# A convolution and MLP backward pass on one Trainium2 core: jobs read operand by operand, a constant burst at the front, diagonals on GpSimd, and new engine orders

## The chip, the core and the metric

The kernel runs on one core of one Trainium2 chip. A core has a matrix engine (TensorE, PE in the profile; its weight loads are PEld), a vector engine (VectorE, DVE), an engine for functions of single elements (ScalarE, ACT), a general one (GpSimd, POOL) and one that here only issues transfers (SyncE, SP). Matmul results arrive in PSUM, everything else lies in SBUF, and DMA engines move data between SBUF and the chip's memory. DMAs are issued from the instruction streams of SP, POOL and ACT, in order. The metric is the time of one execution in microseconds on the device; lower is better. Three runs of the kernel before gave 709.86, 711.56 and 712.73, a median of 711.56 us.

## The reference: what is computed

Two layers of each of two kinds are applied to x = A_q, (S, D) = (2048, 448), F = 1792; then the whole is differentiated. The outputs are the result and the gradients for eight inputs.

```python
def _A_ref(q, k, v, shift_k, ssm_k, ssm_D):
    # k_shift: causal convolution of k over 4 positions, per channel
    kv = k_shift * v
    # y: causal convolution of kv with ssm_k over all 2048 positions, by FFT of length 4096
    y = y + kv * ssm_D
    return q * y

def _B_ref(x, w1, w2):
    return silu(x @ w1) @ w2

x = A_q
x = x + _A_ref(_layernorm(x), A_k, A_v, A_shift_k, A_ssm_k, A_ssm_D)
x = x + _B_ref(_layernorm(x), B_w1, B_w2)
x = x + _A_ref(_layernorm(x), A_k, A_v, A_shift_k, A_ssm_k, A_ssm_D)
x = x + _B_ref(_layernorm(x), B_w1, B_w2)
# outputs: x, and the gradients of A_q, A_k, A_v, A_shift_k, A_ssm_k, A_ssm_D, B_w1, B_w2 for a given grad_out
```

The convolution's result y depends on k, v and the filters alone, so both A layers share one y: it is computed once, ahead of everything that depends on x.

## The kernel before

The work has three parts.

**Head** (`Head.run`, 0 to about 84 us). It computes y. The filter (ssm_k) arrives as four blocks of rows (L364, tiles K_sb and KK), is transposed on TensorE (L427, PSUM tile ps_kt) and copied out; then sixteen pairs of 128x448 matmuls with the Fourier matrix M1 (L456, ps_s) give the first FFT stage, and casts bring the results into A1K. In between, k is transposed (L444, ps_kT), and its 4-tap convolution is done as matmuls (L510) with diagonal matrices, sixteen 112x112 tiles, which VectorE makes from the identity and the taps skc (L414). The FFT of kv, the product and the inverse follow. The copies out of PSUM, of lines L92 (ScalarE) and L94 (VectorE), go to whichever of the two the planner picks.

**Flow** (`Flow.tile`, about 84 to 460 us). Sixteen tiles of 128 rows each go through two MLPs forward and two backward: norm (n0), gate, norm (n1), the turn of n1, up-projection (L663, ps_h), SiLU and its derivative (L700), down-projection (L726, ps_o), norm, gate, norm (n3), the second MLP with output, and then back: gradient up (ps_g), product with the derivative (ghp, ghT), down (ps_n), norm backwards, twice. A tile's stages are spread over many tiles' time, so several tiles are in flight. An operand is "turned" (128 rows by 448 columns transposed) either by two DMA transposes issued on SP (L636, L637) or, for the pairs listed in `ON_PE`, by four TensorE transposes into PSUM (L645) and one copy. The activations and gradients (A0, A1, GH0, GH1) are stored to memory for the weight gradients: A0 and A1 by a DMA transpose and a store on SP (L717, L718), GH0 and GH1 by one store on SP (L711).

**Tail** (from about 460 us). The backward FFT (L875 transposes, L903, L917, L923) gives the gradients for k, v and the filters (`Tail.ends`), interleaved with the weight-gradient jobs (`Tail.jobs`, L1169): for w2 and then w1, seven jobs, each making 256 rows of the gradient as two PSUM accumulations (u = 0, 1) over two layers' operands (gi = 0, 1) and 16 tiles: 64 matmuls. The transposed operand of a job and layer, 1 MB, is loaded on SP into one of three buffers called jb (L1114 for the A arrays, a DMA transpose at L1112 for the GH arrays); the other operands are G and gmov (w2) and two nmov tiles of 16x448 columns (w1), each loaded in two halves at L1095. For most jobs the loop is u outside and gi inside: both operands stay in use until the job's last quarter; three jobs (the last of w2, the first two of w1) run gi outside.

The order of all work is not that of the program text. Every step is registered with a cost per engine that may do it, a priority ("due time") and its dependencies; a planner (`Sched.plan`) simulates the engines with those costs and emits the instructions of each engine in the simulated order. So the constants next to `Flow`, `SKEW` (the distance of the forward and backward stages of a tile), `NUDGE` (shifts of single steps), `TURNED`, `COPIED` (tiles whose first activations are computed from a copy off PSUM) and `NT1`, set the order on every engine. What runs at run time follows that fixed order on each engine, with semaphores between the engines.

```python
both = (which, p) in (("w2", NF // 2 - 1), ("w1", 0), ("w1", 1))
steps = [(u, gi) for gi in range(2) for u in range(2)] if both else [(u, gi) for u in range(2) for gi in range(2)]
```

Of the kernel before, what the change touches and what calls it, by code (L numbers as in the profile page):

```python
# [12 lines left out]
FP32 = mybir.dt.float32  # L13
BF16 = mybir.dt.bfloat16
ACT = mybir.ActivationFunctionType
ALU = mybir.AluOpType
# [4 lines left out]
P = 128  # L21
S = 2048
D = 448
# [3 lines left out]
DC = 112  # L27
ND = 4
NF = 14
# [324 lines left out]
class Head:  # L354
# [11 lines left out]
    def run(self, pr):  # L366
        nc, s, k = self.nc, self.s, self.k
# [7 lines left out]
        dgs = [KK.sub() for h in range(2)]  # L375
# [7 lines left out]
        vs = [V.sub() for _ in range(2)]  # L383
        kt = lambda: KK.t[:, 0, 0:J * D].rearrange("p (j d) -> p j d", d=D)
        kts = [[KK.sub() for _ in range(2)] for _ in range(ND)]
        skb, skc = s.vb("S", "skb", [DC, ND, 4], BF16, "skb"), s.vb("S", "skc", [DC, ND, 4], FP32, "skc")
        Drow = KK.sub(lambda: KK.t[0:1, 1, 13216:13216 + D])
        s.op({"ACT": 0.5}, lambda e: nc.scalar.dma_start(out=skb[:], in_=k.A_shift_k.rearrange("(c p) j -> p c j", p=DC)), w=[skb], prio=pr, dma=("plain", 50e3))
        s.op({"POOL": 0.6}, lambda e: nc.gpsimd.dma_start(out=Drow[:], in_=k.A_ssm_D.rearrange("(o d) -> o d", o=1)), w=[Drow], prio=pr, dma=("plain", 5e3))
        for b in range(4):  # L390
# [17 lines left out]
        s.op({"POOL": 0.3}, lambda e: nc.gpsimd.tensor_copy(skc[:], skb[:]), r=[skb], w=[skc], prio=pr)  # L408
        for h in range(2):

            def dg(e, h=h):
                for c in range(2):
                    for j in range(4):
                        nc.vector.tensor_scalar(out=diag[h]()[:, c, j, :], in0=k.ident[:DC, :DC], scalar1=skc[:, 2 * h + c, j:j + 1], scalar2=None, op0=ALU.mult)  # L414

            s.op({"DVE": 1.3}, dg, r=[skc], w=[dgs[h]], prio=pr + 3 + h)

        pr += 1
        for b in range(4):
            n = 128 if b < 3 else 64  # L420
            for g in range(2):
                pt = s.vb("ps", "d", [P, 8, n], BF16, "ps_kt")

                def tk(e, b=b, g=g, pt=pt, n=n):
                    kv = ksb[b][:].rearrange("p (n1 n2) -> p n2 n1", n2=16)
                    for i in range(8):
                        nc.tensor.transpose(pt[:, i, :], kv[:, 8 * g + i, :], k.ident[:n, :n])  # L427

                s.op({"PE": 0.88}, tk, r=[ksb[b]], w=[pt], prio=s.at(pr + 0.1 * b, b, "kt"))
                c = n / 128  # L430
                s.op({"DVE": 0.07 + 0.54 * c, "ACT": 0.08 + 0.82 * c}, lambda e, b=b, g=g, pt=pt, n=n: _copy(nc, e, kt()[:, 8 * g:8 * g + 8, 128 * b:128 * b + n], pt[:]), r=[pt], w=[kts[b][g]], prio=s.at(pr, b, "kt"))
        s.op({"DVE": 0.35}, lambda e: nc.vector.tensor_tensor(out=kt()[0:1, 0, :], in0=kt()[0:1, 0, :], in1=Drow[:], op=ALU.add),
# [151 lines left out]


T_ = 20.0
SKEW = (8.7, 6.1)
EARLY = 2
ROWS = (0, 128, 256, 320)
TURNED = ((0, 1), (1, 1), (3, 0), (3, 1), (4, 0), (14, 1), (15, 0))  # L590
NUDGE = {(2, "ch"): 0.3, (3, "ch"): 0.9, (4, "ch"): -0.3, (8, "ch"): -1.7, (10, "ch"): -0.7, (2, "cv"): 0.1, (3, "cv"): 0.1, (5, "cv"): 0.4, (7, "cv"): 2, (1, "g"): 8, (15, "g"): 2, (3, "iy"): -2, (7, "iy"): -2, (2, "kt"): 2, (3, "o1"): -12, (0, "o2"): -12, (3, "s2"): -1, (5, "s2"): 1, (6, "s2"): -1.9, (14, "tG"): -8, (0, "tg"): -2, (8, "tk"): 2.4, (6, "tt"): -1, (3, "tv"): 0.2, (5, "tv"): 2, (9, "tv"): -0.4, (11, "tv"): -0.9, (13, "tv"): -1, (1, "w1"): -16, (5, "w1"): 8.5, (6, "w1"): -8, (1, "x3"): 6, (13, "xG"): -4}
NT1 = {1: "nTG", 2: "nT3", 3: "nT3"}
COPIED = (0, 2,)
RAW = ("GH0", "GH1")
ON_PE = ((0, 0), (0, 1), (1, 0), (2, 0), (3, 0), (4, 0), (14, 2), (15, 0), (15, 2))


class Flow:
# [32 lines left out]
    def turn(self, src, pr, tag, on_pe, after=()):  # L631
        nc, k, s = self.nc, self.k, self.s
        if not on_pe:
            nT = self.small(tag, (P, ND, P))
            nT.name = "nT"
            s.op({"SP": 1.2}, lambda e: nc.sync.dma_start_transpose(out=nT[:, 0:3, :], in_=src[:, 0:384]), r=[src], w=[nT], prio=pr - EARLY, dma=("turn", 98e3))  # L636
            s.op({"SP": 1.2}, lambda e: nc.sync.dma_start_transpose(out=nT[:, 3, :], in_=src[:, 320:448]), r=[src], w=[nT], prio=pr - EARLY, dma=("turn", 33e3))  # L637
            return nT
        pt = s.vb("ps", "d", [P, ND, P], BF16, "ps_t")
        nT = self.small(tag, (P, ND, P))  # L640
        nT.name = "nT"

        def mm(e):
            for b, lo in enumerate(ROWS):
                nc.tensor.transpose(pt[:, b, :], src[:, lo:lo + P], k.ident[:])  # L645

        self.last_turn = s.op({"PE": 0.23}, mm, r=[src], w=[pt], prio=pr - EARLY, after=after, hold=[nT])
        s.op({"ACT": 0.62, "DVE": 0.40}, lambda e: _copy(nc, e, nT[:], pt[:]), r=[pt], w=[nT], prio=pr)
        return nT
# [111 lines left out]
    def tile(self, j):  # L761
# [24 lines left out]
        c = b + T_ + SKEW[0]  # L786
        a2, s2 = self.silu(self.turn(n3, at("t3", c + 2.7), "nT3", (j, 1) in ON_PE), 1, at("h2", c + 5.6), (j, 1) not in TURNED)
        up2 = self.last_up
        if j == NT - 1:
            k.lastA = s.vb("J", "lastA", [P, 4, P], BF16, "lastA")  # L790
            k.lastA_op = s.op({"SP": 1.2}, lambda e: nc.sync.dma_start_transpose(out=k.lastA[:], in_=a2[:, 0:4, :].rearrange("p a s -> p (a s)")), r=[a2], w=[k.lastA], prio=c + 10, dma=("turn", 131e3))
# [46 lines left out]
class Tail:  # L838
# [119 lines left out]
    def ends(self, pr):  # L958
# [13 lines left out]
        for i in range(8):  # L972
            py = self.unit([P, 2, 512], name="ps_gkv")

            def mm(e, i=i, py=py):
                bv = B1v[:].rearrange("p a (c n s) -> p a c n s", c=2, n=16)
                for u in range(2):
                    for c in range(2):
                        nc.tensor.matmul(py[:, u, :D].rearrange("p (dh ds) -> p dh ds", ds=4), lhsT=Minv[:, 2 * i + u, c, :], rhs=bv[:, :, c, 2 * i + u, :], start=(c == 0), stop=(c == 1))  # L979

            self.done[1].append(s.op({"PE": 0.76}, mm, r=[B1v, Minv], w=[py], prio=pr + 1))
            gkv = s.vb("P2", "gkv", [P, 2, D], BF16, "gkv")
            sl = slice(2 * i, 2 * i + 2)
            s.op({"ACT": 0.95}, lambda e, py=py, gkv=gkv: nc.scalar.copy(gkv[:], py[:, :, :D]), r=[py], w=[gkv], prio=pr + 1)
            gv = kv[i]
            s.op({"DVE": 0.57}, lambda e, gkv=gkv, gv=gv: nc.vector.tensor_tensor(out=gv[:], in0=gkv[:], in1=gv[:], op=ALU.mult), r=[gkv, gv], w=[gv], prio=pr + 1)
            s.op({"POOL": 0.6}, lambda e, sl=sl, gv=gv: nc.gpsimd.dma_start(out=out3[:, sl, :], in_=gv[:]), r=[gv], prio=pr + 1, dma=("plain", 230e3))
            s.op({"DVE": 0.57}, lambda e, gkv=gkv, sl=sl: nc.vector.tensor_tensor(out=gks[:, sl, :], in0=gkv[:], in1=gks[:, sl, :], op=ALU.mult), r=[gkv, gs[i]], w=[gs[i]], prio=pr + 1)
# [4 lines left out]
        for dc in range(ND):  # L993
            gK = s.vb("P2", "gK", [DC, S], BF16, "gK")
            for g in range(2):
                py = self.unit([P, 8, P], name="ps_gK")

                def mk(e, g=g, py=py, dc=dc):
                    for i in range(8):
                        for c in range(2):  # L1000
                            nc.tensor.matmul(py[:DC, i, :], lhsT=B1k[:, 16 * c + 8 * g + i, dc * DC:(dc + 1) * DC], rhs=Minv[:, 8 * g + i, c, :], start=(c == 0), stop=(c == 1))  # L1001

                self.done[0].append(s.op({"PE": 0.92}, mk, r=[B1k, Minv], w=[py], prio=pr + 3))
                s.op({"ACT": 1.05, "DVE": 1.2}, lambda e, g=g, py=py, gK=gK: _copy(nc, e, gK[:].rearrange("p (n1 n2) -> p n1 n2", n2=16)[:, :, 8 * g:8 * g + 8], py[:DC].rearrange("p i n -> p n i")),
                     r=[py], w=[gK], prio=pr + 3)
            s.op({"POOL": 0.6}, lambda e, dc=dc, gK=gK: nc.gpsimd.dma_start(out=out5[:, dc, :], in_=gK[:]), r=[gK], prio=pr + 3, dma=("plain", 458e3))
            s.op({"DVE": 0.1}, lambda e, dc=dc, gK=gK: nc.vector.tensor_copy(gKD[:, dc:dc + 1], gK[:, 0:1]), r=[gK], w=[gKD], prio=pr + 3)
# [73 lines left out]
    def jobs(self, which, pr):  # L1081
        nc, s, k = self.nc, self.s, self.k
        if which == "w2":
            k.load = []
            gm = s.vb("res", "W1", [P, NT, D], BF16, "gmov")
            gs = [gm.sub() for _ in range(4)]
            gl = [lambda i=i: s.op({"SP": 0.4}, lambda e: nc.sync.dma_start(out=gm[:, 4 * i:4 * i + 4, :], in_=_pm(k.grad_out[0])[:, 4 * i:4 * i + 4, :]), w=[gs[i]], prio=pr - 30, dma=("plain", 458e3), behind=[k.lastA_op]) for i in range(4)]
# [41 lines left out]
        for p in range(NF // 2):  # L1129
# [23 lines left out]
                prev = first[:-2]  # L1153
            if (which, p) == ("w1", 1):
                prev = first[:4]
            both = (which, p) in (("w2", NF // 2 - 1), ("w1", 0), ("w1", 1))
            steps = [(u, gi) for gi in range(2) for u in range(2)] if both else [(u, gi) for u in range(2) for gi in range(2)]
            if split is None:
                split = [(u, gi, range(8 * h, 8 * h + 8)) for u, gi in steps for h in range(2)]
# [212 lines left out]
```

## Time and profile before

| | |
|---|---|
| median of three runs | 711.56 us (709.86 to 712.73) |
| the profiled execution | 713.28 us |
| its span, first to last instruction | 711.4 us |
| mean granted TensorE clock | 0.994 |
| TensorE busy | 684.7 us, 96% |
| VectorE, ScalarE, GpSimd busy | 73%, 57%, 21% |
| head, 26 to 84 us: TensorE, VectorE, ScalarE busy of 57.9 us | 54.99, 53.75, 53.90 |
| flow, 110 to 431 us: the same of 321 us | 321.00, 270.08, 212.55 |
| tail, 612 us to the end: the same of 99.4 us | 93.68, 24.89, 18.94 |

The profile is that of one execution, so the sums made from its rows stand against 713.28 us, of which 1.9 us lie outside the span. A row of a group of instructions has the line, the engine, the operation, out <- in with the program's names and shapes, the count, then the busy time in us and the mean of one in ns, then the idle time of that engine just before them and what ended it. A wait is idle time that ended when the named instruction or DMA signalled. A row of windows has the window, its length, and for each engine the busy time and the count; then the granted clock of TensorE (1.00 is full), the DMA engines' busy share and GB/s. SPq and ACTq mark the time an engine takes to issue a DMA.

### The profile page before, as it was taken

Reading aid. Unit: us, or ns where it says so; the run is one execution under the profiler, and the core shown is the slowest. Engines: PE = TensorE matmul, PEld = TensorE weight load, DVE = VectorE, ACT = ScalarE, POOL = GpSimd, SP = SyncE. Lnnn points to the kernel's source line nnn. Section 1 sums busy time; section 2 is a strip of 40 time slices with the busy share of each in tenths; the row PEclk is TensorE's granted clock in tenths of the full one; section 3 lists DMA queues with packets and bytes.
Section 4 is the critical chain, followed back from the end, with each engine's and each line's share of the span. In section 5 each row is a group of like instructions: output and inputs, shape, how many; then the busy total and the mean of one; then the engine's idle time right before and its main releaser. Section 6 shows DMA issues by size and latency. Waiting matters only on the chain. (4 is left out here: it accounts for less than half of the span.)

```text
span 711.4 us, 18079 instructions
## 1 busy us (share of the span) xinstructions
PE 684.7 (96%) x7491; PEld 474.4 (67%) x7508; DVE 516.9 (73%) x1207; ACT 405.4 (57%) x493; POOL 152.7 (21%) x266
## 2 busy tenths in 40 slices
PE   6999898999999999999999998999999989999996
PEld 4887667777677777677776776656666655555553
DVE  4989798668888888888888875844799776664000
ACT  4989987676667665676656855326865441012311
POOL 1144154103221222222222200030232121000000
PEclk9999999999999999999999999999999999999999
DMA  9979998889788888888788579967599598998871
GB/s 330 262 242 287 354 188 173 192 169 205 168 174 169 181 191 193 191 155 177 178 183 175 136 184 259 285 184 236 163 371 315 171 326 283 233 244 195 181 141 28
DMA packets 277505, 150.64 MB, mean 212 GB/s; under 512 B 224879, under 2 KB 258847, under 8 KB 277037
## 3 DMA queue, kind: packets, MB, share of 16 engines
q1 hardware_dynamic: 263646, 108.42, 66.1%
q0 software_dynamic: 13008, 40.24, 18.6%
q8 instruction: 59, 0.97, 0.6%
q10 hardware_dynamic: 766, 0.80, 0.4%
q14 instruction: 26, 0.20, 0.1%
HBM read 50.68 MB, written 54.60 MB: 148 GB/s over the span
## 5 line engine op out<-in xcount | busy, mean ns | idle before, releaser
L1169 PEld LDWEIGHTS <-jb 128*128 128x128 bf16 x892 | 86.1, 98 | 81.3 <-DMA jb<-A_d 3.2
L92 ACT CAST ghp<-ps_g 128x896 bf16<-128x896 f32 x64 | 58.1, 907 | 60.9 <-PE ps_g L672 50.9
L726 PE MATMUL ps_o<-w2sb,aT 128*128 128x448 bf16 x448 | 89.7, 352 | 0.8 <-ACT aT L700 0.8
L726 PE MATMUL ps_n<-w1T,ghT 128*128 128x448 bf16 x448 | 90.0, 352 | 0.0
L663 PE MATMUL ps_h<-nT,w1sb 128*128 128x128 bf16 x1344 | 86.9, 221 | 3.0 <-DMA nT<-n 2.2
L1169 PE MATMUL ps_d<-nmov,jb 128*128 128x448 bf16 x448 | 87.4, 353 | 0.0
L663 PE MATMUL ps_g<-nT,w2T 128*128 128x128 bf16 x1344 | 85.6, 219 | 0.0
L663 PEld LDWEIGHTS <-w1sb 128*128 128x128 bf16 x1344 | 77.6, 99 | 7.8 <-DMA nT<-n 2.6
L663 PEld LDWEIGHTS <-w2T 128*128 128x128 bf16 x1344 | 77.3, 98 | 7.4
L726 PEld LDWEIGHTS <-aT 128*128 128x128 bf16 x448 | 43.0, 98 | 38.4 <-ACT aT L700 1.0
L726 PEld LDWEIGHTS <-ghT 128*128 128x128 bf16 x448 | 43.1, 98 | 37.8
L700 ACT ACTIVATE aT<-ps_h 128x896 bf16<-128x896 f32 x64 | 56.7, 916 | 19.9 <-PE ps_h L672 11.0
L700 ACT ACTIVATE dT<-ps_h 128x896 bf16<-128x896 f32 x60 | 53.3, 916 | 18.8 <-PE ps_h L672 13.9
L622 POOL TENSOR_TENSOR rstd<-ve,mhalf 128x1 f32<-128x1 f32 x64 | 39.3, 614 | 106.8 <-DVE ve L619 106.7
L750 DVE SCALAR_TENSOR_TENSOR junk<-u,n 128x448 bf16<-128x448 bf16 x64 | 39.9, 624 | 27.1 <-ACT u L828 26.0
L1169 PE MATMUL ps_d<-G,jb 128*128 128x448 bf16 x224 | 47.0, 362 | 2.9 <-DMA jb<-A_d 2.8
L700 ACT ACT_TABLE_LOAD x36 | 46.2, 1283 | 1.2 <-issue 0.6
L1169 PE MATMUL ps_d<-gmov,jb 128*128 128x448 bf16 x220 | 45.4, 353 | 0.0
L92 ACT CAST dob<-ps_d 128x448 bf16<-128x448 f32 x14 | 7.4, 532 | 62.7 <-PE ps_d L1169 62.7
L617 DVE BATCH_NORM_STATS2 st<-x 128x6 f32<-128x448 bf16 x64 | 40.0, 625 | 1.5
L739 DVE TENSOR_TENSOR ghT<-ghp,dT 128x896 bf16<-128x896 bf16 x64 | 39.2, 620 | 0.9 <-ACT ghp L92 0.9
L828 ACT ACTIVATE u<-ps_n,rstd 128x448 bf16<-128x448 f32 x32 | 20.3, 634 | 32.3 <-POOL rstd L622 13.8
(179 smaller groups left out, 1219.4 us busy)
## 6 DMA issues: line engine op xcount, KB each, us to landing
A_d<-turned SPq DMA_DIRECT2D x32, 448.0 KB, 4.1
GH_d<-ghT SPq DMA_DIRECT2D x32, 448.0 KB, 4.3
jb<-A_d SPq DMA_DIRECT2D x12, 1024.0 KB, 8.2
KK<-KK POOLq DMA_DIRECT2D x14, 256.0 KB, 5.4
spec_K<-KK POOLq DMA_DIRECT2D x7, 512.0 KB, 6.0
spec_KV<-X POOLq DMA_DIRECT2D x7, 512.0 KB, 8.9
N_d<-n POOLq DMA_DIRECT2D x32, 112.0 KB, 3.3
sp_c<-spec_KV POOLq DMA_DIRECT2D x14, 256.0 KB, 5.3
```

Of the source, the lines that this page charges most:

```text
L92: nc.scalar.copy(out, in_)
L617: nc.vector.bn_stats(out=st[:], in_=x[:])
L622: s.op({"POOL": 1.0}, lambda e: nc.gpsimd.tensor_tensor(out=rs[:], in0=ve[:], in1=self.k.mhalf[:, 0:1], op=ALU.pow), r=[ve], w=[rs], prio=pr)
L663: nc.tensor.matmul(ps[:, i, :], lhsT=at(b, ft), rhs=nT[:, b, :], **f)
L700: prev = [s.op({"ACT": 0.93}, lambda e, i=i, fun=fun, out=out, late=late: nc.scalar.activation(out[:, 7 * i:7 * i + 7, :], c[:, 7 * i:7 * ...
L726: nc.tensor.matmul(po[:, :D], lhsT=a[:, ft, :], rhs=wt[:, ft * D:(ft + 1) * D], start=(ft == 0), stop=(ft == NF - 1))
L739: s.op({"DVE": 0.57}, lambda e, i=i, t=t: nc.vector.tensor_tensor(out=gh[:, 7 * i:7 * i + 7, :], in0=t[:], in1=d[:, 7 * i:7 * i + 7, :], o ...
L750: nc.vector.scalar_tensor_tensor(out=junk[:], in0=u[:], scalar=1.0, in1=n[:], op0=ALU.mult, op1=ALU.mult, accum_out=cp[:, 1:2])
L828: s.op({"ACT": 0.85}, lambda e: nc.scalar.activation(u[:], pn[:, :D], ACT.Identity, scale=r[:], accum_out=cp[:, 0:1]), r=[pn, r], w=[u, cp ...
L1169: nc.tensor.matmul(ps[:, :D], lhsT=rows(t, gi, u), rhs=at(t), start=(first and t == ts[0]), stop=(last and t == ts[-1]))
```

## The change

Seven things are changed.

- At the front of TensorE's work stand nine 128x448 matmuls on a tile of ones, which VectorE fills; their result is not read.
- The sixteen diagonals are made on GpSimd, in four registered steps, and not on VectorE in two.
- `SKEW`, `TURNED`, `NUDGE`, `NT1` and the planner's cost of the filter's transposes have new values; `COPIED` takes tile 1 in.
- `ON_PE`: tile 13's n1 and tile 15's n3 are turned on TensorE, and tile 15's n1 by DMA.
- The first w2 load is given a dependency on the last tile's turn of n3, or none if that turn is on TensorE.
- The steps that compute gkv and gK reserve their output buffer when the matmul is ordered, not when its copy is.
- All jobs run with gi outside: both PSUM accumulations take all of the first operand, then all of the second.

```diff
+        one = s.vb("S", "A1K", [P, D], BF16, "one")
+        s.op({"DVE": 0.2}, lambda e: nc.vector.memset(one[:], 1.0), w=[one], prio=pr - 1)
+        pw = s.vb("ps", "d", [P, 512], FP32, "ps_w")
+
+        def warm(e):
+            for _ in range(9):
+                nc.tensor.matmul(pw[:, :D], lhsT=one[:, 0:P], rhs=one[:], start=True, stop=True)
+
+        s.op({"PE": 3.36}, warm, r=[one], w=[pw], prio=pr - 1)
...
+        skb.since = 4.6
...
-            def dg(e, h=h):
-                for c in range(2):
+            for c in range(2):
+
+                def dg(e, h=h, c=c):
                     for j in range(4):
-                        nc.vector.tensor_scalar(out=diag[h]()[:, c, j, :], in0=k.ident[:DC, :DC], scalar1=skc[:, 2 * h + c, j:j + 1], scalar2=None, op0=ALU.mult)
-
-            s.op({"DVE": 1.3}, dg, r=[skc], w=[dgs[h]], prio=pr + 3 + h)
+                        nc.gpsimd.tensor_scalar(out=diag[h]()[:, c, j, :], in0=k.ident[:DC, :DC], scalar1=skc[:, 2 * h + c, j:j + 1], scalar2=None, op0=ALU.mult)
+
+                s.op({"POOL": 1.2}, dg, r=[skc], w=[dgs[h]], prio=pr + 2.5 + h)
...
-                s.op({"PE": 0.88}, tk, r=[ksb[b]], w=[pt], prio=s.at(pr + 0.1 * b, b, "kt"))
+                s.op({"PE": 0.48}, tk, r=[ksb[b]], w=[pt], prio=s.at(pr + 0.1 * b, b, "kt"))
...
-SKEW = (8.7, 6.1)
+SKEW = (7.3, 5.4)
...
-TURNED = ((0, 1), (1, 1), (3, 0), (3, 1), (4, 0), (14, 1), (15, 0))
-NUDGE = {(2, "ch"): 0.3, (3, "ch"): 0.9, (4, "ch"): -0.3, (8, "ch"): -1.7, (10, "ch"): -0.7, (2, "cv"): 0.1, (3, "cv"): 0.1, (5, "cv"): 0.4, (7, "cv"): 2, (1, "g"): 8, (15, "g"): 2, (3, "iy"): -2, (7, "iy"): -2, (2, "kt"): 2, (3, "o1"): -12, (0, "o2"): -12, (3, "s2"): -1, (5, "s2"): 1, (6, "s2"): -1.9, (14, "tG"): -8, (0, "tg"): -2, (8, "tk"): 2.4, (6, "tt"): -1, (3, "tv"): 0.2, (5, "tv"): 2, (9, "tv"): -0.4, (11, "tv"): -0.9, (13, "tv"): -1, (1, "w1"): -16, (5, "w1"): 8.5, (6, "w1"): -8, (1, "x3"): 6, (13, "xG"): -4}
-NT1 = {1: "nTG", 2: "nT3", 3: "nT3"}
-COPIED = (0, 2,)
+TURNED = ((0, 1), (1, 1), (4, 1), (14, 1), (15, 0), (15, 1))
+NUDGE = {(2, "ch"): 0.3, (8, "ch"): -1.7, (5, "cv"): 0.4, (1, "h2"): -2, (3, "iy"): -2, (7, "iy"): -1, (5, "s2"): 1, (14, "tG"): -8, (8, "tk"): 2.4, (3, "tv"): 0.2, (5, "tv"): 2, (13, "tv"): -1, (5, "w1"): 8.5, (6, "w1"): -8, (0, "xG"): 2, (13, "xG"): -4}
+NT1 = {3: "nT3"}
+COPIED = (0, 1, 2,)
 RAW = ("GH0", "GH1")
-ON_PE = ((0, 0), (0, 1), (1, 0), (2, 0), (3, 0), (4, 0), (14, 2), (15, 0), (15, 2))
+ON_PE = ((0, 0), (0, 1), (1, 0), (2, 0), (3, 0), (4, 0), (13, 0), (14, 2), (15, 1), (15, 2))
...
-            s.op({"SP": 1.2}, lambda e: nc.sync.dma_start_transpose(out=nT[:, 3, :], in_=src[:, 320:448]), r=[src], w=[nT], prio=pr - EARLY, dma=("turn", 33e3))
+            self.last_rows = s.op({"SP": 1.2}, lambda e: nc.sync.dma_start_transpose(out=nT[:, 3, :], in_=src[:, 320:448]), r=[src], w=[nT], prio=pr - EARLY, dma=("turn", 33e3))
...
+        k.load = [] if (j, 1) in ON_PE else [self.last_rows]
...
-            self.done[1].append(s.op({"PE": 0.76}, mm, r=[B1v, Minv], w=[py], prio=pr + 1))
             gkv = s.vb("P2", "gkv", [P, 2, D], BF16, "gkv")
+            self.done[1].append(s.op({"PE": 0.76}, mm, r=[B1v, Minv], w=[py], prio=pr + 1, hold=[gkv]))
...
-                self.done[0].append(s.op({"PE": 0.92}, mk, r=[B1k, Minv], w=[py], prio=pr + 3))
+                self.done[0].append(s.op({"PE": 0.92}, mk, r=[B1k, Minv], w=[py], prio=pr + 3, hold=[gK]))
...
         if which == "w2":
-            k.load = []
...
-            both = (which, p) in (("w2", NF // 2 - 1), ("w1", 0), ("w1", 1))
+            both = True
```

## The prediction

> **What bounds the kernel now.** I read the page's busy line first, then TensorE's waits, then windows around each wait, and last the single instructions there. The page:
>
> ```profile
> PE 684.7 (96%) x7491; PEld 474.4 (67%) x7508; DVE 516.9 (73%) x1207; ACT 405.4 (57%) x493; POOL 152.7 (21%) x266
> ```
>
> TensorE is the bound: 26.7 us of the 711.4 are not busy. The matmuls that the change leaves in place cannot become fewer, so the change can win only what stands beside them: waits, and time in which matmuls run at half clock. The waits of TensorE (total, times, longest):
>
> ```profile
> PE ps_kt L427 <- DMA K_sb<-in_A_ssm_k_dram: 4.5, 1, 4.5
> PE ps_d L1169 <- DMA jb<-A_d: 2.8, 1, 2.8
> PE ps_v L923 <- DVE pq L917: 2.2, 4, 0.9
> PE ps_h L663 <- DMA nT<-n: 2.2, 1, 2.2
> ```
>
> Windows around them (length, busy time of each engine, then PEclk):
>
> ```profile
> 10.76:17.31 6.55, 6.13 (x31) 3.49 (x31) 4.08 (x5) 3.63 (x5) 0.00 (x0) 1.00 1.02 417
> 17.31:26.10 8.79, 8.79 (x114) 7.09 (x113) 8.44 (x10) 7.84 (x10) 0.00 (x0) 1.00 1.21 276
> 431.60:433.77 2.17, 0.02 (x1) 0.00 (x1) 1.20 (x4) 0.72 (x2) 0.00 (x0) 0.99 1.03 270
> 433.77:437.15 3.38, 3.38 (x36) 2.88 (x37) 3.13 (x10) 0.00 (x0) 0.00 (x0) 0.50 1.21 275
> 583.92:586.71 2.79, 0.00 (x1) 0.00 (x1) 2.79 (x7) 0.74 (x1) 1.14 (x2) 1.00 1.21 294
> 587.34:590.75 3.41, 3.41 (x11) 1.38 (x10) 3.13 (x4) 0.00 (x0) 0.00 (x0) 0.50 1.03 348
> ```
>
> Both long waits are followed by one stretch of 3.4 us at clock 0.50, so each costs its length and half of that stretch, 1.7 us, again. The start is slow too, though no PEclk row says it: six L456 matmuls start 0.37 us apart at 11.76 to 13.97 and 0.19 us apart at 18.08 to 19.22. By these durations the clock was half until about 17.3.
>
> [...]
>
> **1. Head.** The change puts nine 128x448 matmuls on a constant ahead of everything on TensorE, moves 16 diagonal products (L414) from VectorE to GpSimd, and leaves the rest in nearly the old order. TensorE does nothing until the first load lands at 4.5. GpSimd's first memset starts at 0.24, and SP's and ScalarE's first entries stand at 0.74; with a VectorE memset the nine can start by about 1.2 and take 9 x 0.37 = 3.3 us: they end at about 4.6 and cost nothing. What they can change is when the clock is released. The half-clock stretches lie on one grid of 3.41 us; laid back to the start it gives 7.07, 10.49, 13.90 and 17.31. TensorE was 85% busy with gaps in the two stretches ending at 10.49 and 13.90 (not released), full in that ending at 17.31 (released). In the new kernel the stretch 3.66 to 7.07 is full: the end of the nine, then transposes of the rows landed at 4.48 and 6.00. I expect release at 7.07. VectorE, without the diagonals, also evacuates from the first transposes on:
>
> ```profile
> L94 DVE CAST A1K<-ps_s 128x896 bf16<-128x896 f32 x8 | 8.5, 1088 | 2.5 <-PE ps_s L456 2.4
> L94 DVE COPY KK<-ps_kT 112x1024 bf16<-112x1024 bf16 x5 | 3.4, 685 | 0.2
> L414 DVE TENSOR_SCALAR KK<-ident,skc 112x112 bf16<-112x112 bf16 x16 | 2.6, 246 | 4.9 <-POOL skc L408 4.9
> ```
>
> The first L456 cannot start before M1 lands at 10.76 (now 11.76). After it 16 casts (0.93 on ScalarE, 1.09 on VectorE) and 8 ps_kT copies (1.03 and 0.69) remain, about 10.5 us for two engines. At full clock they are the bound, so the last one ends at about 21.5 to 22.4 (now 26.06): **-3.5**, between -1 and -4.5. After 17.3 both engines are over 90% busy up to 86, so the gain is carried to the flow. The diagonals have no row on GpSimd. The nearest are these:
>
> ```profile
> L408 POOL CAST skc<-skb 112x16 f32<-112x16 bf16 x1 | 0.2, 196 | 1.5 <-DMA skb<-in_A_shift_k_dram 1.5
> L622 POOL TENSOR_TENSOR rstd<-ve,mhalf 128x1 f32<-128x1 f32 x64 | 39.3, 614 | 106.8 <-DVE ve L619 106.7
> ```
>
> 16 of them cost 3.2 to 9.8 us from 4.9 on and end by 15; their reader (L510) starts at 24.65 now and about 21 then. Cost 0; it shows only if one takes over 1.0 us.
>
> **2. Flow.** Its start (84 to 110 us) has four waits of 0.8 to 1.85 us; TensorE's order is the same there. Tile 1's copy off PSUM is new (two 1.09 us casts on VectorE), with 1.8 us of other work moved out of its way: 0, within 1 either way. From 110 to 431 TensorE is 321.00 of 321.00 us busy, so nothing can be won, only lost, and here the new order takes risks. For tiles 6 to 12, 14 and 15 the GH0 store of the tile four before (L711) now stands ahead of the two DMA turns of n1 on SP; before it stood behind. The chain from the end of that tile's ps_g: cast 0.9 and product 0.6 for the second half with their hand-overs (2.3 to 2.6), store issue 0.5 to 1.05, turns 1.25 and 1.25 to 1.7, landing 1.4 to 3.2 after the last issue. That makes 7 to 9 us, against 8.5 us of matmuls in between (ps_h 2.95, ps_n 2.65, ps_g 2.95). So between 1.5 us of slack and a 0.7 us wait per tile (n1's turns landed 1.4 to 5.2 us early before). I take 0.2 us for each of nine tiles: **+2**, between 0 and +8. Waits under 1.85 us cost no clock: that gap at 106.75 was followed by none.
>
> **3. The wait at 431.6.** Tile 15's n3 is ready at 421.75, but SP is in other work:
>
> ```profile
> 420.04 3.65 SPq L717 DMA_TRANSPOSE turned<-aT  x1
> 423.78 0.60 SPq L1114 DMA_DIRECT2D jb<-A_d  x1
> 424.43 4.38 SPq L636 DMA_TRANSPOSE nT<-n  x1
> ```
>
> The two halves of the turn land at 433.73 and 434.07; TensorE is there at 431.6. In the changed kernel tile 15's n3 is turned on TensorE (four transposes and a copy of 0.4 to 0.7), ready by about 427, nearly 5 us early. That takes away 2.16 us, 1.7 us of half clock, and adds 0.25 us of transposes: **-3.6**. Next in line is tile 14's G2 turn (slack about 1.1 us), so this could shrink to -2.5.
>
> The words "first w2 load behind the last turn" do nothing: the code sets that dependency to an empty list when the last turn is on TensorE, which it is. Cost 0.
>
> **4. FFT stage, 500 to 560.** The L923 waits on VectorE's L917 (0.9 longest) stay; filler matmuls cover perhaps one of the two large ones (0.78): **-0.4**, within 1.
>
> **5. Jobs operand by operand, 560 to the end.** Each jb buffer is now read by 32 matmuls in a row and freed after half a job. The 2.79 us wait is for the load of job 5's second operand, issued at 571.64 and landed at 586.67, on DMA engines that are over 100% full (1.21 above). In the changed order that load is issued 5 us ahead of its old place and is needed 22 us after issue: the wait goes (2.79 + 1.7 = 4.5, and some 0.7 of small waits: -5.2). But both pairs of nmov loads (917 KB each) now stand on SP ahead of job 6's first operand, where one pair did. It issues 23 us after job 4's remaining half begins, needs 9.4 + 8.1 us of pairs to drain and 5.4 to 7.1 for itself: landing at 38.5 to 40 against a need at 36.1. So a wait of 2.4 to 4 comes, in part with clock lost: **-1.3**, between -5.2 and +2. From the first GH0 operand on (98.5 us to the end) there are the same matmuls and the same last evacuations.
>
> **Sum.** -3.5 + 0 + 2 - 3.6 - 0.4 - 1.3 = -6.8. The profiled execution took 713.28 us, 0.24% over the median of 711.56; its successor should take 706.5, and the median 704.8.
>
> **Rivals.**
> - *Clock not released early* (13%). If the constant burst lies badly on the grid, or the gaps between loads (VectorE and ScalarE still free the two PSUM slots) throttle it again, only the freed VectorE and a shorter cold stretch remain, -1.25 in place of -3.5: 707.1. For it: the unreleased stretches were 85% busy. Against: a stretch that was 70% transposes, 491.77 to 495.18, stayed at full clock.
> [...]
> - *n1's turn behind the GH0 store, half a microsecond late* (16%). 0.4 to 0.9 us at nine tiles is 4 to 8: 707 to 711.5, mostly no change.
> - *The same turn, well late: slower* (10%). The store moves 448 KB, and its median time to landing is 4.3 us by the page; if the turns' small packets queue behind all of it, they land 4.3 us after issue, the chain grows to 9.9 to 10.5 us and each of nine tiles waits 1.4 to 2.0: +13 to +18 where I have +2. 716, up to 721. It decides from about 1.4 us of wait per tile. For it: the store is issued just ahead on the same queue. Against: DMA is 0.84 busy from 110 to 431, and n1's turns landed in 1.4 to 3.2 us among such stores.
> - *The change doesn't do what it says* (6%): operand by operand only moves the wait to job 6's load, with the whole loss of clock, +2 for step 5: 708.1.
>
> **How the numbers follow.** Forecast 704.8, chance 55%, own range 700 to 708. What a measurement of this kernel can tell from no change is about 0.5%, 3.6 us: faster is under 708.0, slower over 715.1. Faster: 55 + 7 (half of the clock rival) + 3 + 3 = 68%. Slower: 10 + 1 = 11%. Same: 21%. The range: step 5's low bound alone gives 700.9, with a little of the head's 700; above, step 2's +8 and step 5's +2 come to 714, and 712.5 leaves out the slower rival and a little more.
>
> **What would show it.** Right: the first L456 at about 10.8 with starts 0.19 us apart and the last A1K cast before 22.5; no half clock near 432; no wait for job 5's jb, one for job 6's first operand of 2 to 4 us; ps_h waits on nT in the flow of under 3 us in all. Wrong: L456 0.37 us apart after 10.8 (clock); a row "ps_h <- DMA nT" with eight or more waits of over 0.5 us between 180 and 400 (turns behind the store); diagonals on GpSimd still running at 21; a clock of 0.50 anywhere after 600.

## The result, and the profile after

The changed kernel is slower by 0.8%: 715.22 us (median of 20 runs, 711.82 to 721.27) against 709.69 (20 runs, 706.49 to 714.23), ratio 1.0079, 95% interval 1.0061 to 1.0096. The forecast was 704.8 and "faster". A ratio, here and below, is to the kernel before, measured in the same session; a time is the median of the runs. The two first profiles do not show the loss, since that of the changed kernel is the fastest of its 20 runs (711.8 us) and that of the kernel before lies near the top of its own (713.3). Two profiles taken by chance showed -1.5 us where the medians differ by +5.5. So each kernel was profiled again, and everything below is read from several executions. The ratios leave out slow runs, those over 1.5% above the fastest of their kernel; the profiled executions of `e2_old_head` and `g4_old_head_turn_first` are such runs, so their waits are not used, and so are two of the six runs of `g3_turn_first`, which its median still includes.

The page's busy line and TensorE's longest waits (total, times, longest) of the changed kernel:

```profile
PE 683.6 (96%) x7503; PEld 473.7 (67%) x7521; DVE 515.1 (73%) x1192; ACT 413.7 (58%) x501; POOL 166.1 (23%) x282
```

```profile
PE ps_v L557 <- DVE pq L552: 3.2, 4, 2.0
PE ps_v L935 <- DVE pq L929: 2.2, 4, 0.9
PE ps_t L656 <- DVE n L634: 2.2, 1, 2.2
PE ps_h L674 <- DMA nT<-n: 2.0, 2, 1.3
...
PE ps_w L392 <- DVE one L387: 1.4, 1, 1.4
```

The 4.5 us wait for K_sb has gone (the burst fills it, from 1.38 to 4.92 us), and the two long waits that the prediction priced, at 432 and 584 us, are not there. New are a wait of the head's last stage on VectorE's product (L552) and waits of ps_h on n1's turn in the flow. A second profile of the same kernel (`e1_after_again`, 720.2 us) shows how far the first of them goes:

```profile
PE ps_v L557 <- DVE pq L552: 7.0, 2, 6.5
PE ps_gD L1025 <- DVE gKD L1019: 2.3, 1, 2.3
PE ps_t L656 <- DVE n L634: 2.2, 1, 2.2
PE ps_h L674 <- DMA nT<-n: 2.1, 2, 1.8
```

The best single marker is the start of the flow, the first matmul of L663 (L674 in the changed kernel), on tile 0. It stands at 93.9, 93.1, 93.1 and 94.0 us in four profiles of kernels with the old head (mean 93.5), and at 97.3, 101.9, 99.4, 98.3, 99.9 and 98.8 in six with the new one (mean 99.3). In these executions the new head starts the flow 5.7 us later, as much as the whole result; by times, the next section puts its share at 4.2.

### The profile page after: what moved, and what is told of

The parts are those of the page before. It is cut to its first block, busy times and chain, and to the rows that moved or that the text cites. A ratio compares the mean times of both kernels' runs of the same rounds, so it can differ in the third digit from the quotient of the medians.

```text
span 710.0 us, 18116 instructions
## 1 busy us (share of the span) xinstructions
PE 683.6 (96%) x7503; PEld 473.7 (67%) x7521; DVE 515.1 (73%) x1192; ACT 413.7 (58%) x501; POOL 166.1 (23%) x282
## 5 line engine op out<-in xcount | busy, mean ns | idle before, releaser
L674 PE MATMUL ps_h<-nT,w1sb 128*128 128x128 bf16 x1344 | 85.8, 219 | 2.8 <-DMA nT<-n 2.0
L674 PE MATMUL ps_g<-nT,w2T 128*128 128x128 bf16 x1344 | 85.6, 219 | 0.0
L674 PEld LDWEIGHTS <-w2T 128*128 128x128 bf16 x1344 | 77.6, 98 | 8.6
L674 PEld LDWEIGHTS <-w1sb 128*128 128x128 bf16 x1344 | 76.6, 98 | 7.3 <-issue 3.2
L633 POOL TENSOR_TENSOR rstd<-ve,mhalf 128x1 f32<-128x1 f32 x64 | 43.6, 681 | 87.5 <-DVE ve L630 86.9
L711 ACT ACTIVATE dT<-ps_h 128x896 bf16<-128x896 f32 x58 | 51.2, 915 | 11.6 <-PE ps_h L683 7.6
L1180 PE MATMUL ps_d<-G,jb 128*128 128x448 bf16 x224 | 45.2, 353 | 0.1
```

The source lines that it names most:

```text
L633: s.op({"POOL": 1.0}, lambda e: nc.gpsimd.tensor_tensor(out=rs[:], in0=ve[:], in1=self.k.mhalf[:, 0:1], op=ALU.pow), r=[ve], w=[rs], prio=pr)
L674: nc.tensor.matmul(ps[:, i, :], lhsT=at(b, ft), rhs=nT[:, b, :], **f)
L711: prev = [s.op({"ACT": 0.93}, lambda e, i=i, fun=fun, out=out, late=late: nc.scalar.activation(out[:, 7 * i:7 * i + 7, :], c[:, 7 * i:7 * ...
L1180: nc.tensor.matmul(ps[:, :D], lhsT=rows(t, gi, u), rhs=at(t), start=(first and t == ts[0]), stop=(last and t == ts[-1]))
```

## The experiments

### Which of the three parts loses?

One part at a time was put back into the changed kernel; the changed kernel itself ran beside them.

> The changed kernel, unchanged, once more. Its first profile (711.8 us) lay 3.4 us under its median and the one of the kernel before 3.6 us over its own, so the two profiles do not show the 5.5 us that the medians differ by. Every theory: 5 us (0.7%) over the kernel before, and the flow starts (first L663 of the flow, 93.9 us before, 97.3 after) at 97 again if the head is the cause. Theory head: the head alone gives 3.4 of the 5 us. Theory flow: the rest comes from waits of ps_h on the turn of n1 between 180 and 400 us, of which the first profile had one tile (1.3 and 0.7 us) and this one should have several. Theory jobs: it comes from a wait for jb after 560 us (0.9 us in the first profile).

Measured: 717.49 us, ratio 1.0085 (1.0052 to 1.0117). The flow starts at 101.9 us and not at 97. The waits on n1's turn are again those of one tile (2.1 us in all), and no wait for a jb reaches 0.3 us.

```diff
# e2_old_head: Head.run and the shifts of its steps as before
...
-        s.op({"PE": 3.36}, warm, r=[one], w=[pw], prio=pr - 1)
...
-                        nc.gpsimd.tensor_scalar(out=diag[h]()[:, c, j, :], ...
+                        nc.vector.tensor_scalar(out=diag[h]()[:, c, j, :], ...
```

> The head as before (no constant burst, diagonals on VectorE, the old shifts of the head's steps), flow and jobs as changed. Theory head: the flow starts at 93.9 us again, 3.4 us earlier than in the changed kernel, and the time falls by 3 to 4 us, to 0.2% over the kernel before. Theories flow and jobs: the flow may start earlier, but what follows keeps its loss, at least 4 us over the kernel before.

Measured: 712.33 us, ratio 1.0026 (0.9993 to 1.0059). About 4 us of the loss go with the head.

```diff
# e3_old_flow: the flow's constants as before
-SKEW = (7.3, 5.4)
+SKEW = (8.7, 6.1)
-ON_PE = (... (13, 0), (14, 2), (15, 1), (15, 2))
+ON_PE = (... (14, 2), (15, 0), (15, 2))
# and TURNED, NT1, COPIED, the flow's NUDGE entries
```

> The flow's constants as before (SKEW, TURNED, its shifts, NT1, COPIED, ON_PE), head and jobs as changed. Theory flow (n1's turns behind the GH0 stores): no wait of ps_h on n1's turn between 180 and 400 us, the 2.2 us wait at about 432 us comes back with its half clock, and the time is still 2 to 4 us below the changed kernel. Theory head: the flow starts at 97 and the time stays 5 us over the kernel before, or 3 us more for the wait at 432.

Measured: 713.69 us, ratio 1.0029 (1.0002 to 1.0055). No wait on nT in the flow, and none at 432 us either, although the old `ON_PE` is back. The flow's change costs about 4 us.

```diff
# e4_old_tail: the jobs, their shift (1, "w1"): -16, and gkv, gK as before
...
-            both = True
+            both = (which, p) in (("w2", NF // 2 - 1), ("w1", 0), ("w1", 1))
```

> The jobs and the gkv and gK steps as before (u outside, gi inside for most jobs), head and flow as changed. Theory jobs: 2 us or more below the changed kernel. Theories head and flow: the wait for job 5's operand comes back (2.8 us and 1.7 us of half clock) and the time is 0 to 4 us above the changed kernel.

Measured: 715.94 us, ratio 1.0077 (1.0051 to 1.0103), the same as the changed kernel. The jobs are not the loss; head and flow both are, each by about the same amount. One expectation was missed: the wait for job 5's operand did not come back. The only wait for a jb in this profile is 1.0 us long, at 610 us.

### The head: why is its gain not carried on?

VectorE's longest waits between 40 and 95 us, first in the kernel before, then in the second profile of the changed kernel:

```profile
DVE t L628 <- ACT Ysb L92: 4.2, 1, 4.2
DVE A1kv L94 <- PE ps_s L526: 1.3, 1, 1.3
```

```profile
DVE pq L552 <- DMA KK<-KK: 7.3, 1, 7.3
```

The fourth product of the last FFT stage waits for a move of half a tile of KK, issued on GpSimd (L569, L558 before). The two kernels issue the last eight moves (four column ranges, two halves each) in different orders: before, columns 4096 to 6143 first; changed, after both halves of 8192 to 10239 and one of 10240 to 12287. The fourth product needs 4096 to 6143. In the changed kernel these two moves are the fourth and fifth of eight. The issues of the moves on GpSimd, in the kernel before and in the second profile of the changed one:

```profile
56.58 1.04 POOL L558 DMA_DIRECT2D KK<-KK  x2 [1.48 <-ACT KK L92]
```

```profile
54.90 2.62 POOL L569 DMA_DIRECT2D KK<-KK  x5 [0.34 <-PE ps_s L494]
```

Before, the pair was issued at 56.6 and 57.1 us and landed by 61.8. In the changed kernel the fifth move was issued at 55.7 us in the first profile and at 57.0 in the second, and landed at 67.9 and 73.8, behind the other moves; the product started 0.1 us later each time. In all six executions with this head and order VectorE waits 2.6 to 7.3 us for that move, and a later product 0.6 to 2.4 us more for the store KS_d<-ks, which shares its buffers. When the entries of `NUDGE` that the change drops are taken out of the kernel before one at a time, the planner gives this order for one entry only, (7, "cv"): +2, the last convolution step. Two experiments turn on that entry alone, and two on the head's code.

```diff
# f2_conv7_late: the changed kernel
-NUDGE = {..., (13, "xG"): -4}
+NUDGE = {..., (13, "xG"): -4, (7, "cv"): 2}
# f3_conv7_early: the kernel before
-NUDGE = {..., (5, "cv"): 0.4, (7, "cv"): 2, (1, "g"): 8, ...}
+NUDGE = {..., (5, "cv"): 0.4, (1, "g"): 8, ...}
```

> The changed kernel with one number put back: the shift of +2 on the last convolution step of the head, (7, cv). In the planned order of GpSimd it puts the pair of moves of KK's columns 4096 to 6143 back ahead of those of columns 8192 and up. Theory move order: VectorE's fourth product (L552) no longer waits 2.7 to 7.3 us for a move, the flow starts at 90 to 92 us (97 to 102 in the changed kernel), and the time falls by 4 to 6 us, to that of the kernel before. Rival, DMA bound: the moves land no earlier since the burst's head start has only put Minv and w1 among them, the flow starts at 95 or later, and the time stays 4 us or more over the kernel before.

Measured: 712.35 us, ratio 1.0029 (1.0005 to 1.0052): 3 to 4 us less than the changed kernel, as the move order demands, but the flow starts at 97.4, not at 90 to 92. The wait for the move is gone. The convolution now ends at 65.4 us in place of 52.9, and other waits stand where that one was. This is half a hit: the time of the expectation came, its flow start did not, and 97.4 is no earlier than the earliest start without the entry (97.3).

> The kernel before with only that shift, (7, cv): +2, left out: the pair of moves goes behind three moves of later columns, as in the changed kernel, with no constant burst. Theory move order: a wait of VectorE's product for a move appears, 2 us or more, the flow starts at 96 to 98 us and the time is 2 to 5 us over the kernel before. Rival, DMA bound by the earlier head: without the burst nothing changes, 0 within 1 us.

Measured: 713.65 us, ratio 1.0042 (1.0016 to 1.0068), flow start 96.1. Without any burst, one entry less costs 3.0 us (0.42%), about what the flow starts later (2.6). The rival "the earlier head floods the DMA engines" is out as the only cause. The wait itself is smaller than expected: the product that needs the moved pair starts at 70.28 us, 0.1 us after the fifth move's landing at 70.16, but VectorE was idle for only 1.2 us before it (the profile puts this idle time down to a matmul). The entry also changes the order of VectorE's products and of other steps, so the 3.0 us are the price of the entry, not of the moves alone.

```diff
# f4_head_code: the kernel before with the new Head.run, all NUDGE entries as before
...
+        s.op({"PE": 3.36}, warm, r=[one], w=[pw], prio=pr - 1)
...
-            s.op({"DVE": 1.3}, dg, r=[skc], w=[dgs[h]], prio=pr + 3 + h)
+                s.op({"POOL": 1.2}, dg, r=[skc], w=[dgs[h]], prio=pr + 2.5 + h)
...
-                s.op({"PE": 0.88}, tk, r=[ksb[b]], w=[pt], prio=s.at(pr + 0.1 * b, b, "kt"))
+                s.op({"PE": 0.48}, tk, r=[ksb[b]], w=[pt], prio=s.at(pr + 0.1 * b, b, "kt"))
# g2_burst_alone: the kernel before with the burst only
...
+        s.op({"PE": 3.36}, warm, r=[one], w=[pw], prio=pr - 1)
```

> The kernel before with the head's code of the changed kernel alone: the constant burst, the diagonals on GpSimd, the planner's cost of the filter's transposes; all shifts as before, so that the moves stand in the old order. Theory move order: the head's 3 us come through, the flow starts at 90 to 91.5 us and the time is 2 to 3.5 us under the kernel before (0.3 to 0.5%). Rival, DMA bound: the stage from 40 to 85 us is bound by its transfers, the flow starts at 93 us or later and the time is that of the kernel before.

Measured: 712.32 us, ratio 1.0034 (1.0016 to 1.0052), flow start 94.5. My theory failed here: the moves stand in the old order and no product waits for a DMA, and yet the 2 us by which the convolution starts earlier (22.0 for 23.8 and 24.6) are lost before the flow begins, and about 1 us more.

The stage from the first convolution to the first ps_y, in the kernel before, in the changed one and in its second profile, one answer each (window, length, busy times, then PEclk, DMA share, GB/s):

```profile
24.65:86.68 62.03, 57.91 (x817) 49.27 (x826) 55.56 (x76) 57.45 (x72) 22.67 (x39) 1.00 0.94 294
```

```profile
21.90:90.08 68.18, 60.15 (x816) 50.39 (x826) 55.72 (x74) 58.41 (x74) 22.60 (x39) 0.97 0.91 277
```

```profile
23.20:94.60 71.40, 61.22 (x825) 51.48 (x825) 55.81 (x74) 58.24 (x74) 22.67 (x39) 0.95 0.85 262
```

The work is the same (DVE 55.6 to 55.8, ACT 57.5 to 58.4 us busy, but for some missing records the same number of matmuls); the stage is 6 to 9 us longer, because every engine idles more, and part of it runs at half clock (70.51 to 73.92 us in the first profile, 73.13 to 79.96 in the second; PEclk 0.97 and 0.95 over the whole stage). In `f4_head_code` it is 65.2 us. What is left to explain the loss is the order. No run kept the old order with the diagonals on GpSimd, so for the part of `f4_head_code` this is argued, not shown. A planner that is told of an earlier start and other costs gives every later step of the stage another place, and this stage had been within 4 us of TensorE's busy time.

> The kernel before with only the burst of nine matmuls ahead of it; every engine's order is otherwise that of the kernel before, step for step. Theory A: the head's clock gain is real but the stage up to 85 us is bound by the engines' order and the transfers, the last ps_kT comes 1 to 2 us earlier, the flow starts at 92.5 to 93.5 us and the time is within 1 us. Theory B, of the forecast: the gain is carried through, flow start at 90.5 to 91.5, time 2 to 3 us under the kernel before. Then it is the new order of the head, not a bound, that ate it.

Measured: 710.28 us, ratio 1.0005 (0.9983 to 1.0026). Here every engine keeps its order, and nothing is lost: the flow starts at 92.6. But nothing clear is won either. Another execution with this head (`h2_tail_burst`, below) starts its flow at 93.6, and the old head without the burst does so at 93.1 to 94.0. Theory A was nearer. The mean granted clock of the profiled execution was 0.994, no higher than in the two of the kernel before (0.994 and 0.998).

### The flow: what do the waits on n1's turn come from?

Four profiles with the changed flow have 2.0, 2.1, 3.3 and 3.7 us of these waits between 125 and 425 us; six with the old flow and the old or new head have 0, and two with the burst ahead of the old head and flow 0.5 and 1.0. The SP issues before the wait of 1.3 us at 271.3 us in the first profile of the changed kernel:

```profile
263.71 0.34 SPq L729 DMA_DIRECT2D A_d<-turned  x1
264.15 0.39 SPq L722 DMA_DIRECT2D GH_d<-ghT  x1
264.65 3.43 SPq L647 DMA_TRANSPOSE nT<-n  x1
268.13 2.10 SPq L648 DMA_TRANSPOSE nT<-n  x1
```

It looks just like the rival in the prediction: two stores of 448 KB, then the first turn, which takes 3.43 us to issue where it takes 1.25 elsewhere. So the stores were put behind the turns.

```diff
# g3_turn_first: in Flow.tile of the changed kernel
+            self.late[j + 4] = self.store(gh1, "GH0", j, d + 20)
...
+        if j in self.late:
+            self.late[j].behind.append(self.last_rows)
# g4_old_head_turn_first: the same, with the old head
```

> The changed kernel with the GH0 store of four tiles before put back behind the two turns of n1 on SP for tiles 5 to 15; the orders of TensorE, ScalarE and GpSimd are the same. Theory: the waits of ps_h on nT between 170 and 400 us (2.0 to 3.7 us in five profiles) fall under 0.7 us in all and the time by 2 to 3 us, to 713. Rival: the turns wait for the DMA engines whatever stands ahead, and nothing changes.

Measured: 721.38 us, ratio 1.0128 (1.0079 to 1.0176). The waits stayed, 3.4 us in five places, with every turn of n1 ahead of the store, and the delayed SP brought a new one:

```profile
PE ps_d L1186 <- DMA gmov<-in_grad_out_dram: 6.5, 1, 6.5
```

> The changed kernel with the old head and with the turns of n1 ahead of the GH0 stores: both losses undone, flow and tail else as changed. Theory: flow start at 93.5 us, no waits on nT, time 1.5 to 3.5 us under the kernel before. Rival: the tail's gain is not there or the flow has another loss, and the time is that of the kernel before.

Measured: 716.71 us, ratio 1.0096 (1.0066 to 1.0126). The order of turn and store is not the cause. SP issues one after the other, and paid for the stores that were held back: the loads of gmov went out at 464.4 us in `g3_turn_first`, 450.9 in the changed kernel.

What the traces do show is when VectorE finishes n1. From there to TensorE's use of the turn it is 9.1 to 9.3 us for tiles 5 to 14 in the kernel before; in the changed one it is 5.3 to 6.3 for eight of the ten tiles from 5 on that are turned by DMA. In VectorE's order n1's normalisation stands ahead of both ghT products of the tile four before in the old kernel, and behind them in the new. `SKEW` sets the distance between those two stages.

```diff
# h1_old_skew: the changed kernel; h4_oldhead_oldskew: the same with the old head
-SKEW = (7.3, 5.4)
+SKEW = (8.7, 6.1)
```

> The changed kernel with only SKEW put back to (8.7, 6.1). In VectorE's order this puts n1's normalisation back ahead of the ghT products of the tile four before, and the turns ahead of the GH0 store. Theory late n1: in the profiles n1 is normalised 5.3 to 6.3 us before TensorE needs its turn in the changed kernel, 9.3 us in the kernel before, and that is what the waits on nT come from; here it is over 8 us for tiles 6 to 12, the nT waits between 170 and 400 us fall under 0.7 us in all, and the time falls by 2 to 3 us, to 713 (the head's loss stays). Rival, another part of the flow (ON_PE, COPIED, TURNED): the waits and the time stay at 715 to 716.

Measured: 712.58 us, ratio 1.0019 (0.9995 to 1.0043), with no nT wait at all between 125 and 425 us and 9.3 us or more from n1 to its use. The head's long stage is still there (flow start 98.8). Against the changed kernel's ratios (1.0079 and 1.0085) that is 4.3 to 4.7 us, as much as `e3_old_flow` gained with all the flow's constants. `SKEW` moves other stages too; that it works through n1 is the reading that the waits and the 9.3 us support, together with `g3_turn_first`, where SP's order alone did not help.

> The changed kernel with the old head and the old SKEW: the losses of the head and of the late n1 both undone, COPIED, ON_PE, TURNED and the tail as changed. Theory late n1: flow start at 93.5 us, nT waits under 0.7 us in all, no wait for gmov at 463 us, and the time is 2 to 3 us under the kernel before, like the new tail alone. Rival: what is left of the flow's changes loses by itself, 1 us or more over the new tail alone (708.5).

Measured: 708.76 us, ratio 0.9964 (0.9941 to 0.9987), flow start 94.0, no nT wait and no wait for gmov at 463 us. Nothing else in the flow's change loses by more than the intervals.

### The two waits that I had priced, and the jobs

> The kernel before, unchanged, for a second profile: its first one (713.3 us) lay well above its median. Theory of the lost head: the flow starts at 93.5 to 94 us again, without a wait of over 1 us between 60 and 85 us. My forecast took 3.6 us for the wait at 432 us and 4.5 us for the one at 584: if they are part of every execution they stand here again, each with its stretch at half clock; if the forecast priced two accidents of one profile, at least one of them is missing and the time is about 710.

Measured: 711.09 us, ratio 1.0006 (0.9985 to 1.0027), the profiled execution 708.7. TensorE's first waits in it:

```profile
PE ps_kt L427 <- DMA K_sb<-in_A_ssm_k_dram: 4.6, 1, 4.6
PE ps_d L1169 <- DMA jb<-A_d: 3.9, 2, 3.2
PE ps_v L923 <- DVE pq L917: 2.2, 4, 0.9
PE ps_t L645 <- DVE n L623: 1.8, 1, 1.8
```

The wait on nT at 432 us is not among them: it is 0.49 us long, and the mean granted clock of this execution is 0.998, as against 0.994 in the first. In five other executions with this flow it is 0.56 (`f3_conv7_early`), 0.31 (`f4_head_code`), 0.64 (`g2_burst_alone`), under 0.25 (`g1_new_tail`) and 1.28 (`h2_tail_burst`). SP's order up to there is the same each time, but the turn that took 4.38 us to issue in the first profile took 2.59 in this one. I had priced one bad draw. The wait for job 5's operand is in all five executions with the old flow and the old jobs (2.79, 3.16, 3.09, 2.74 and 2.84); in the first profile a stretch at clock 0.50 follows it, from 587.34 to 590.75 us.

```diff
# g1_new_tail: the kernel before with the new jobs, without their shift (1, "w1"): -16, gkv and gK held
...
-            both = (which, p) in (("w2", NF // 2 - 1), ("w1", 0), ("w1", 1))
+            both = True
# h2_tail_burst: the same, and the burst of nine matmuls
```

> The kernel before with only the tail changed: all jobs operand by operand, gkv and gK with their buffers held. Theory: the wait for job 5's jb (2.7 to 3.2 us in four profiles of the old tail) goes, one of 1 to 2 us comes for job 6, and the time is 2 to 3.5 us under the kernel before; a version that beats both. Rival: the DMA engines are full there and the wait only moves, 0 within 1 us.

Measured: 708.55 us, ratio 0.9976 (0.9954 to 0.9998), so 1.7 us less, with an interval that reaches from 0.1 to 3.3. Its only wait for a jb:

```profile
PE ps_d L1169 <- DMA jb<-A_d: 1.8, 1, 1.8
```

It is 1.8 us at 592, on another operand than before; the mean granted clock of this execution is 0.998.

> The kernel before with the new tail and the burst of nine matmuls, all other orders as before: the two parts that did not lose by themselves. If they add up, 2 to 3 us under the kernel before (0.3 to 0.4%), the flow starting at 92.6 us. Rival: the half us that the burst brings is lost in the wait for tile 0's n3 at 108 us, which at 2.15 us can cost a stretch of half clock: then the time is that of the new tail alone, 708.5, or up to 1 us more.

Measured: 708.33 us, ratio 0.9957 (0.9930 to 0.9985). It is the best version found, 0.4% under the kernel before; it does not differ from `h4_oldhead_oldskew` or from the new tail alone by more than the intervals. Its profile does not show the two gains that were to add up: the flow starts at 93.6 us and not at 92.6, and the wait for a jb, on the same operand as in `g1_new_tail`, is 3.0 us, as long as in the kernel before, at a mean granted clock of 0.997:

```profile
L1178 PE MATMUL ps_d<-gmov,jb 128*128 128x448 bf16 x220 | 45.1, 353 | 3.0 <-DMA jb<-A_d 3.0
```

## Why the prediction was wrong

**Step 1, the head, is the step that failed.** Its first half was roughly right: full clock came at 5.66 us in the first profile of the changed kernel, as against 17.31 in that of the kernel before, the diagonals on GpSimd took 0.56 us each and ended at 14, and nobody waited for them. The release that was expected at 7.07 us rested on the grid of one execution; in the first profile of the changed kernel the grid lies 1.4 us earlier. But the first L456 stayed at 11.3 to 12.1 (10.8 forecast), the last A1K cast came at 23.4 to 24.7 against 24.4 to 25.6 (21.5 to 22.4 forecast), so 1 us was won there and not 3.5. Then came the two sentences that decided the case: that the change "leaves the rest in nearly the old order", and that "both engines are over 90% busy up to 86, so the gain is carried to the flow". High busy shares say that a stage is tight; they don't say that it can be shifted as it stands. The planner does not shift a stage, it makes a new one. The forecast looked at the head's first 26 us and not at the new order from 26 to 86 us, where the term was not -3.5 but +5.7 by the start of the flow and +4.2 by times (`e2_old_head`): one missing entry put the move of columns 4096 to 6143 behind three others (3.0 us by itself, `f3_conv7_early`), the new code and costs lose the earlier start and 1 us more (`f4_head_code`), and the rest comes with the two together, partly as half clock (3.41 and 6.83 us of it in the two profiles of the changed kernel, between 70 and 80 us). No rival had it.

**Step 3** was mis-sized by taking one execution for the kernel: -3.6 forecast, where 0 to -1.3 was to be had in the six executions that do not have the bad draw. **Step 2** had the place, the sign and nearly the size of the flow's loss (+2 forecast; waits of 2.0 to 3.7 us, about 4 us in time), and the wrong reason: not the store ahead of the turn, but n1 normalised 3 to 4 us later on VectorE because of `SKEW`. I had seen that VectorE's order was turned round and put it down as a detail of the chain. **Step 5** forecast -1.3. With the jobs alone it is -1.7 (0.1 to 3.3 less), and the wait moved to another operand as forecast. In the changed kernel the old jobs are no slower (`e4_old_tail`), and the forecast wait of 2.4 to 4 us is 0.9 in one profile and absent in the other. So the agreement in size is partly luck; and the landing at 38.5 to 40 us on which that wait rests cannot be had from the terms shown beside it. **Step 4** (-0.4 forecast) was of the right small size: the waits on L917 and L929 are 2.2 us in the kernel before and 2.2 and 1.5 in the two profiles of the changed one; the empty dependency of the first w2 load did nothing, as said.

Put together by times, the head costs 4.2 us (`e2_old_head`), the flow 4.0 to 4.7 (`e3_old_flow`, `h1_old_skew`) and the jobs bring between -0.6 and 1.7 (`e4_old_tail`, `g1_new_tail`): 6.5 to 9.5, against 5.5 measured for the whole. Each of these is a difference of two ratios with intervals of 0.2 to 0.3% (1.5 to 2 us) on either side, so the parts add up within their errors and no closer. Two things stay open. One is a wait of TensorE on VectorE's gKD in the tail (L1025), 2.3 us in the second profile of the changed kernel and 3.0 in `h1_old_skew`, but 0.2 in the first. The other is which of the other dropped shifts or costs would let the new head keep its earlier start; `f2_conv7_late` shows that the one entry is not enough. Of the rivals, "the clock not released early" did not come true in the first profile of the changed kernel: see the last section.

## What to carry to other kernels

When a change alters the inputs of a planner or the order on an engine, forecast the whole stage from its new order, the moves and small DMAs included; a gain at a stage's front counts only if the order behind it is unchanged or has been followed through. Measure how long before its use an operand is ready, engine by engine, in both orders: 9.3 us against 5.3 told what the list of waits, and an obvious store in the queue, did not. Don't price a wait from one profile; two microseconds that one execution shows may be a draw, and a second profile of the same kernel costs less than an explanation.

## What the runs showed of the hardware

The burst brought full clock earlier. In the first profile of the changed kernel its matmuls start 0.37 us apart from 1.73 to 4.34 us, TensorE is busy without a gap from 2.25 to 5.66, full clock is granted from 5.66 on, and the first six matmuls of L456 (L467 there), at 11.70 to 12.64, start 0.19 us apart. In that of the kernel before the same six, at 11.76 to 13.60, start 0.37 us apart; TensorE was busy for 2.91 us of 7.07 to 10.49 and 2.95 us of 10.49 to 13.90, without a release, and for all of 13.90 to 17.31, and full clock is granted from 17.31 on. In the changed kernel the early release held over the transposes and the gaps between them: TensorE was busy for 2.20 us of 5.66 to 9.07 and for 2.63 us of 9.07 to 12.48, and the first stretch at clock 0.50 begins at 70.51.

The length of a wait alone does not tell whether half clock follows. In these two profiles tile 0's wait for n3 was 1.85 us in the kernel before and 2.16 us in the changed one, and neither was followed by it. After a wait of 1.96 us in the changed kernel, which ended at 69.30, a stretch at 0.50 begins at 70.51; where those of 2.16 and 2.79 us in the kernel before end, at 433.77 and 586.71, such stretches begin at 433.74 and 587.34. Each is 3.41 us long. In each of the two profiles the release and the starts of these stretches lie on one grid of 3.41 us. TensorE was busy for 1.46 us of the last stretch of the grid before half clock in the changed kernel (67.10 to 70.51), and for 1.29 and 0.63 us in the kernel before (430.33 to 433.74, 583.93 to 587.34); in the stretches that hold most of tile 0's wait, with full clock after them, for 1.56 us before (106.06 to 109.47) and 1.54 changed (108.06 to 111.47). Five waits do not set a limit.
